# GpSimd subtracts the minimum and one exponential does two tiles, in a fused attention and MLP kernel

## The chip, the cores and the metric

The kernel runs on one core of one Trainium2 chip. The metric is the device time of one execution, in microseconds (us), as the median of several runs. A core has five engines that work side by side, each with its own queue of instructions, and that wait for each other through semaphores: TensorE (PE, matmuls; PEld is its loading of weights), VectorE (DVE), ScalarE (ACT), GpSimd (POOL) and SyncE (SP, here only an issuer of DMAs).

## The reference

A transformer block with 2048 tokens of width 640 that is modulated by a condition vector: attention with 32 heads of width 128 against a cache of 2048 keys and values, then a mixer and an MLP. Only the attention is touched by the change. Cut to it:

```
q = (x @ wq).reshape(B, Sq, H, Dh).transpose(0, 2, 1, 3)
scores = einsum('bhqd,bhkd->bhqk', q, k_cache) * Dh ** -0.5
p = softmax(scores, axis=-1)
o = einsum('bhqk,bhkd->bhqd', p, v_cache)
return o.transpose(0, 2, 1, 3).reshape(B, Sq, H * Dh) @ wo
```

The output projection, two layer norms, the mixer and the MLP follow. They are the same in both kernels.

## The kernel before, in words

The program is recorded operation by operation in a class `Prog`. Each operation names its engine, what it reads and what it writes; from that `Prog` derives the waits, also between two operations of one engine of which the second reads what the first wrote (VectorE, ScalarE, GpSimd). Each engine runs its operations strictly in the order in which they were recorded, so the order is the one written in the loop below.

The attention loop has one step `s` for each tile of 128 queries of one head: 16 tiles a head, 32 heads, 512 tiles. In one step:

- TensorE makes the scores of tile `s`, 128 x 2048, in two halves (`qk`, L301 and L15), into one PSUM area `Sps` of 2048 columns. There is no second such area: a half is made again for the next tile as soon as VectorE has read it. Between the halves TensorE multiplies the transposed probabilities of an earlier tile, `s - PVD`, by the values (`pv`, L314), and does a piece of other work: the next head's queries (`q_piece`, L246) or transposes of probabilities (`t_piece`, L262). Such pieces go into one of two PSUM banks in turn (`Oaug`, `QPp`). The list `PIECES` places the query pieces; `PE_STEPS` names the few tiles of a head whose probabilities TensorE transposes and from which step on (tiles 3 and 10 in a head of kind 0; tiles 2, 3 and 10 in kind 1, each fourth head). All others are transposed by a DMA (`transpose`, L231), mostly two tiles at a time.
- VectorE copies each half from PSUM into a score slot in SBUF (`negS`, L594), scaled by minus 1/sqrt(128), and keeps the minimum of each row. There are three slots: tile `s` uses slot `s % 3`, so it must wait until the reader of tile `s - 3` is done.
- GpSimd takes the smaller of the two halves' minima (L604, one column).
- ScalarE makes the probabilities in one instruction, exp(minimum - slot) with the minimum as its bias, from float32 into a bfloat16 ring of 10 tiles (`Pb`, L607).
- ScalarE also copies the product of two tiles out of PSUM (L585, in each second step), the queries (`q_evac`, L253) and the transposes made by TensorE (`t_evac`, L271). In each step these are recorded ahead of the exponential. `by_dve` gives the second half of some of the transposes to VectorE instead (L273): of tile 3 in every head, and of tile 2 in heads of kind 1, 40 copies in all.
- GpSimd takes reciprocals of the row sums for four tiles (`rcp`, L455), scales one tile (`norm`, L462), and for each fourth tile issues a DMA of the result to a scratch (L469).

`PVD` is the distance in steps between a tile's scores and its product with the values, 8 here. L585 is in the step in which the later tile of a pair has its product, an odd step with a `PVD` of 8. The line numbers are those of the profile of the kernel before; in the changed kernel lines behind the edits move down (L594 becomes L596, L604 L606, the plain exponential L619; the new pass is L610 and the new exponential L616).

The waits around the change are set by these keys of `Prog`:

```
r=[("S", half)], w=[("negS", s % 3), ("nmh", half, r8)])
...
r=[("negS", s % 3), ("nm", r8)], w=[("Pb", s % RP)])
```

The first is VectorE's copy into the slot, the second the exponential that reads it.

Of the kernel before, what the change touches and what calls it, by code (L numbers as in the profile page):

```python
# [7 lines left out]
ACT = mybir.ActivationFunctionType  # L8
# [115 lines left out]
def bass_adaLN_cond__mha_block_cached__mixer_s_mlp__prompt_kernel(  # L124
# [7 lines left out]
    NQT = SQ // 128  # L132
# [13 lines left out]
    with ExitStack() as es:  # L146
# [11 lines left out]
        if True:  # L158
            with ExitStack() as es1:
                sb1 = lambda name, shape, dt: es1.enter_context(nc.sbuf_tensor(name, shape, dt))  # L160
                RP = 10
                PVD = 8
                PE_STEPS = ({3: 6, 10: 13}, {2: 5, 3: 7, 10: 14})
                kind = lambda h: 1 if h % 4 == 1 else 0
                US = KT * (SQ + 4)
                sb1("pad", [128, 32], F32)
                ring = sb1("ring", [128, 2 * RP, SK], BF16)
                negS = sb1("negS", [128, 3, SK], F32)
                wo = sb1("wo", [128, H, D], BF16)
                kv = sb1("kv", [128, 2 * SK + 2 * NKT * 130 + 2 * KT * 128 + 2 * SQ], BF16)  # L170
                small = sb1("small", [128, 4 * NQT + 32], F32)
                hTx = sb1("hTx", [128, US], BF16)
                Of = sb1("Of", [128, 4, 2, 130], F32)
# [4 lines left out]
                nm0, nm1, nm, rl = [small[:, 4 * NQT + 8 * i:4 * NQT + 8 * i + 8] for i in range(4)]  # L178
# [8 lines left out]
                Pb = ring[:, 0:RP]  # L187
# [22 lines left out]
                G = Prog(nc, es1, "a")  # L210
# [61 lines left out]
                    else:  # L272
                        G.op("vector", lambda v: v.tensor_copy(dst, src), r=[("J", jb)], w=[("PT", g % RP, r)])  # L273

                by_dve = lambda g, r: r == 1 and g % NQT in (2, 3)
                PIECES = []
                for steps in PE_STEPS:
                    taken = [u for j in steps.values() for u in range(2 * j, 2 * j + 4)]
# [68 lines left out]
                if H > 1:  # L347
# [8 lines left out]
                     r=["id0"], w=["ident"])  # L356
# [3 lines left out]
                for k in range(KT):  # L360
                    G.op("gpsimd", lambda g, k=k: g.tensor_scalar(out=s_bc[:, k, :], in0=ones_f, scalar1=c_f[:, k:k + 1],
                                                                  scalar2=1.0, op0=ALU.mult, op1=ALU.mult),
                         r=["onesf", "cf"] + WRK, w=[("sbc", k)])
# [52 lines left out]
                def q_head0(cc):  # L416
                    for q in range(KT):
                        q_piece(0, cc, q)
                    q_evac(0, cc)
# [22 lines left out]
                def mod_rows(i):  # L442
                    n0, n1 = MROW[i]
                    bank = PO[:, (i % 2) * 512:(i % 2) * 512 + n1 - n0]

                    def f(t):
                        for k in range(KT):
                            ins = t.matmul(bank, s_bc[:, k, :], wmodr[:, k, n0:n1], start=(k == 0), stop=(k == KT - 1))
                        return ins
                    G.op("tensor", f, r=[("sbc", k) for k in range(KT)] + [("wm", 1)] + WRK, w=[("O", i % 2)])  # L450
                    G.op("scalar", lambda a: a.copy(mod_bc[:, n0:n1], bank), r=[("O", i % 2)], w=[("mod", i)])
# [35 lines left out]
                w2 = negb[:, 2 * H * 128:2 * H * 128 + KT * D].rearrange("p (k n) -> p k n", k=KT)  # L487
                us = hTx[:, 0:US].rearrange("p (k q) -> p k q", k=KT)
                nT = kv[:, 0:KT * SQ].rearrange("p (t k q) -> p t k q", t=NQT, k=KT)
# [61 lines left out]
                LAG = 4  # L551
                for s in range(NG + PVD + LAG):
                    h, j = divmod(s, NQT)
                    g_ = s - PVD
                    evacs = []
                    if s <= 2:
                        for i in ((0,), (1, 2), range(3, len(MROW)))[s]:
                            mod_rows(i)
                    if s == 3:
                        G.op("gpsimd", lambda g: g.tensor_scalar(  # L560
                            out=mod_bc[:, 2 * D:3 * D], in0=mod_bc[:, 2 * D:3 * D], scalar1=1.0, scalar2=1.0, op0=ALU.add, op1=ALU.mult),
                            r=[("mod", i) for i in range(len(MROW))], w=["mod"])
                    for half in range(2):
                        if s < NG:
                            qk(s, half)
                        if half == 0 and s in (NG + PVD - 5, NG + PVD - 4):
                            b0 = a_pe(0, None if s == NG + PVD - 5 else b0, (s - NG - PVD + 5,))
                        if half == 0 and s == NG + PVD - 2:
                            b1 = a_pe(1, None, (0,))
                        if 0 <= g_ < NG:  # L570
                            pv(g_, half)
                        if s == 0 and half == 1:
                            q_head0(NQC - 1)
                        if h + 1 < H and 2 * j + half in PIECES[kind(h)]:
                            cc, q = PIECES[kind(h)][2 * j + half]
                            q_piece(h + 1, cc, q)
                            if q == KT - 1:
                                evacs.append((q_evac, h + 1, cc))
                        for g, r in t_of(s):
                            t_piece(g, r, half)  # L580
                            if half == 1:
                                evacs.append((t_evac, g, r))
                    if 0 <= g_ < NG and g_ % 2 == 1:
                        p = g_ // 2
                        G.op("scalar", lambda a, p=p: a.copy(  # L585
                            Of[:, p % 4].rearrange("p z d -> p (z d)")[:, 0:259], PO[:, (p % 2) * 512:(p % 2) * 512 + 259]),
                            r=[("O", p % 2)], w=[("Of", p % 4)])
                    for fn, x, y in evacs:
                        if fn is q_evac or not by_dve(x, y):
                            fn(x, y)  # L590
                    for half in range(2):
                        if s < NG:
                            r8 = s % 8
                            G.op("vector", lambda v, half=half, s=s, r8=r8: v.tensor_scalar(  # L594
                                out=negS[:, s % 3, half * 1024:(half + 1) * 1024],
                                in0=Sps[:, half * 1024:(half + 1) * 1024],  # L596
                                scalar1=-SCALE, scalar2=None, op0=ALU.mult, op1=ALU.min,
                                accum_out=(nm0 if half == 0 else nm1)[:, r8:r8 + 1]),
                                r=[("S", half)], w=[("negS", s % 3), ("nmh", half, r8)])
                    for fn, x, y in evacs:  # L600
                        if fn is t_evac and by_dve(x, y):
                            fn(x, y)
                    if s < NG:
                        G.op("gpsimd", lambda g, r8=r8: g.tensor_scalar(  # L604
                            out=nm[:, r8:r8 + 1], in0=nm0[:, r8:r8 + 1], scalar1=nm1[:, r8:r8 + 1], scalar2=None, op0=ALU.min),
                            r=[("nmh", 0, r8), ("nmh", 1, r8)], w=[("nm", r8)])  # L606
                        G.op("scalar", lambda a, s=s, r8=r8: a.activation(  # L607
                            Pb[:, s % RP, :], negS[:, s % 3, :], ACT.Exp, bias=nm[:, r8:r8 + 1], scale=-1.0),
                            r=[("negS", s % 3), ("nm", r8)], w=[("Pb", s % RP)])
                        if not is_pe(s):  # L610
                            if s % 2 == 1 and not is_pe(s - 1):
                                transpose(s - 1, 2)
                            elif s % 2 == 1 or is_pe(s + 1):
                                transpose(s, 1)
                        if j == 2 and h >= 1 and h + 1 < H:
                            load_k(h + 1)  # L616
                        if h + 1 == H and j in (2, PVD + 1):
                            i = 0 if j == 2 else 1
                            load_ot(0, OTC[i], OTC[i + 1], i)  # L619
                        if j == 6 and h + 2 < H:  # L620
                            load_wq(h + 2)
                        if j == PVD + 1 and h + 1 < H:
                            load_v(h + 1)
                    if 0 <= s - PVD - LAG:
                        gr, z = divmod(s - PVD - LAG, 4)
                        if z == 0:
                            rcp(gr)
                        norm(gr, z)
                    if s == NG:
                        G.op("gpsimd", lambda g: g.memset(mhalf, -0.5), w=["mhalf"] + NEG)  # L630
                        load_ot(0, OTC[2], OTC[3], 2)
                        load_xt(0, 1)
                        load_ot(1, 0, H // 2, 0)
                        load_ot(1, H // 2, H, 1)
                    if s == NG + 2:
                        load_xt(1, NQC)
# [57 lines left out]
                for n in range(KT):  # L694
                    lst = []
                    p = 0
                    while p < 128:
# [8 lines left out]
                        p = pe_  # L706
# [203 lines left out]
```

## Time and profile before

| | before |
|---|---|
| median of 3 runs | 1574.27 us |
| lowest, highest run | 1574.03, 1575.15 us |
| profiled execution: span, first to last instruction | 1568.9 us |
| busy, TensorE matmuls | 1472.3 us (94%) |
| busy, TensorE weight loads | 923.4 us (59%) |
| busy, VectorE | 1398.3 us (89%) |
| busy, ScalarE | 1275.9 us (81%) |
| busy, GpSimd | 623.0 us (40%) |
| mean granted TensorE clock | 0.998 |
| first and last L594 | start at 35.4 and 1250.6 us |

The profile is of one execution on the chip. For the profiled execution the record holds its span alone, from its first instruction to its last; the median of the runs is 5.4 us longer, and this rest lies around the span. The shares are means over the whole span: the attention loop takes it up to about 1252 us, and the output projection, the mixer and the MLP, in which ScalarE is nearly idle, take what is left. Neighbouring instructions of one engine overlap by some tenths of a microsecond, so what an instruction costs its engine is the distance between two starts rather than its own duration. A group's line ends with the idle time of its engine just before such instructions, and with what ended that idle time.

### The profile page before, as it was taken

Reading aid. Unit: us, or ns where it says so; the run is one execution under the profiler, and the core shown is the slowest. Engines: PE = TensorE matmul, PEld = TensorE weight load, DVE = VectorE, ACT = ScalarE, POOL = GpSimd, SP = SyncE. Lnnn points to the kernel's source line nnn. Section 1 sums busy time; section 2 is a strip of 40 time slices with the busy share of each in tenths; the row PEclk is TensorE's granted clock in tenths of the full one; section 3 lists DMA queues with packets and bytes.
Section 4 is the critical chain, followed back from the end, with each engine's and each line's share of the span. In section 5 each row is a group of like instructions: output and inputs, shape, how many; then the busy total and the mean of one; then the engine's idle time right before and its main releaser. Section 6 shows DMA issues by size and latency. Waiting matters only on the chain.

```text
span 1568.9 us, 33553 instructions
## 1 busy us (share of the span) xinstructions
PE 1472.3 (94%) x13947; PEld 923.4 (59%) x13175; DVE 1398.3 (89%) x2471; ACT 1275.9 (81%) x1121; POOL 623.0 (40%) x1396
## 2 busy tenths in 40 slices
PE   5899999999999999999999999999999899999999
PEld 3466666666665566566656666566566655554545
DVE  6999999999999999999999999999999937667435
ACT  4999999999999999999999999999999900034230
POOL 0144444444444444444444444444444433323100
PEclk9999999999999999999999999999999999999999
DMA  9999999999999999999999999999999999725100
GB/s 298 239 221 239 237 242 237 233 241 243 237 240 233 239 232 232 240 236 235 229 237 236 233 243 249 226 242 243 235 241 237 238 246 190 157 53 144 38 22 34
DMA packets 1172828, 334.59 MB, mean 213 GB/s; under 512 B 1153280, under 2 KB 1166656, under 8 KB 1172672
## 3 DMA queue, kind: packets, MB, share of 16 engines
q1 hardware_dynamic: 1164192, 311.30, 100.8%
q0 software_dynamic: 6144, 16.79, 3.5%
q10 hardware_dynamic: 2336, 4.34, 0.8%
q8 instruction: 108, 1.77, 0.5%
q14 instruction: 48, 0.39, 0.1%
HBM read 43.48 MB, written 19.40 MB: 40 GB/s over the span
## 4 chain that ended last, share of the span: by engine, by line
ACT 40%; DVE 23%; PE 19%; DMA 9%; issue 7%; POOL 1%; POOLq 0%; DVEq 0%
ACT ring L607 32%; DVE negS L594 20%; DMA ring<-ring 8%; PE Sps L540 8%; PE Sps L847 4%; ACT ring L271 3%; ACT kv L253 2%; ACT Of L585 2%; PE QPp L798 2%; PE Oaug L798 2%; DVE ring L273 1%; PE Sps L783 1%; DVE ring L379 1%; DMA negS<-o_scratch 1%; PE PTp L314 1%
## 5 line engine op out<-in xcount | busy, mean ns | idle before, releaser
L594 DVE TENSOR_SCALAR_CACHE_REDUCE negS<-Sps 128x1024 f32<-128x1024 f32 x1024 | 1177.7, 1224 | 19.4 <-PE Sps L15 18.5
L607 ACT ACTIVATE ring<-negS,small 128x2048 bf16<-128x2048 f32 x512 | 1045.7, 2066 | 13.7 <-POOL small L604 12.5
L314 PEld LDWEIGHTS PTp<-kv,ring 128*128 128x128 bf16 x8192 | 554.1, 98 | 325.0 <-issue 69.6
L314 PE MATMUL PTp<-kv,ring 128*128 128x129 bf16 x8192 | 645.3, 220 | 25.0 <-DMA ring<-ring 23.9
L15 PE MATMUL Sps<-kv 128*128 128x512 bf16 x1024 | 387.9, 379 | 16.8 <-DVE negS L594 9.9
L604 POOL TENSOR_SCALAR small<-small 128x1 f32<-128x1 f32 x512 | 146.4, 286 | 621.8 <-DVE negS L594 621.7
L301 PE MATMUL Sps<-kv 128*128 128x512 bf16 x919 | 354.3, 386 | 27.8 <-DVE negS L594 16.5
L462 POOL TENSOR_SCALAR On<-Of,small 128x128 bf16<-128x128 f32 x512 | 191.0, 373 | 13.0
L301 PEld LDWEIGHTS Sps<-kv 128*128 128x128 bf16 x1024 | 98.1, 96 | 141.7 <-DVE negS L594 121.6
L455 POOL TENSOR_TENSOR small<-Of,small 128x4 f32<-128x4 f32 x128 | 133.1, 1040 | 8.8 <-ACT Of L585 8.7
L469 POOL DMA_DIRECT2D o_scratch<-On x128 | 103.1, 806 | 40.8 <-POOL On L462 37.2
L585 ACT COPY Of<-PTp 128x259 f32<-128x259 f32 x256 | 108.6, 424 | 13.2 <-PE PTp L314 13.2
L246 PE MATMUL Oaug<-hTx,kv 128*128 128x512 bf16 x268 | 101.9, 385 | 3.7 <-DVE hTx L411 3.7
L246 PE MATMUL QPp<-hTx,kv 128*128 128x512 bf16 x259 | 97.7, 382 | 2.6 <-ACT hTx L406 2.1
L728 ACT ACT_TABLE_LOAD x1 | 1.3, 1283 | 112.6 <-POOL hTx L746 112.6
L594 DVE DVE_READ_ACCUMULATOR negS<-Sps 128x1 f32 x1024 | 90.3, 88 | 0.0
L271 ACT COPY ring<-Oaug 128x1024 bf16<-128x1024 bf16 x72 | 77.0, 1069 | 0.0
L641 POOL TENSOR_SCALAR negS<-negS 128x1 f32<-128x1 f32 x48 | 24.2, 504 | 125.2 <-DVE negS L650 125.2
L540 PE MATMUL Sps<-wo,negS 128*128 128x128 bf16 (+1 forms) x503 | 69.9, 298 | 1.2 <-DMA negS<-o_scratch 0.8
L540 PE MATMUL Sps<-wo,hTx 128*128 128x512 bf16 (+1 forms) x502 | 69.3, 297 | 0.5
L851 DVE TENSOR_TENSOR ring<-Sps,ring 128x640 f32<-128x640 f32 x15 | 12.4, 824 | 59.5 <-PE Sps L847 59.5
L655 DVE TENSOR_TENSOR ring<-Sps,mod_bc 128x640 f32<-128x640 f32 x16 | 13.1, 821 | 53.6 <-PE Sps L540 32.9
(88 smaller groups left out, 1052.7 us busy)
## 6 DMA issues: line engine op xcount, KB each, us to landing
kv<-in_A_v_cache_dram SPq DMA_DIRECT2D x32, 512.0 KB, 5.0
o_scratch<-On POOLq DMA_DIRECT2D x128, 128.0 KB, 4.7
kv<-in_A_wq_dram SPq DMA_DIRECT2D x32, 160.0 KB, 3.2
wo<-in_A_wo_dram SPq DMA_DIRECT2D x1, 5120.0 KB, 16.5
ring<-ring SPq DMA_TRANSPOSE x248, 7.1
ring<-in_A_x_dram SPq DMA_DIRECT2D x5, 640.0 KB, 6.6
ring<-in_w_mod_dram SPq DMA_DIRECT2D x1, 3200.0 KB, 13.8
out_dram<-wo SPq DMA_DIRECT2D x15, 160.0 KB, 1.8
```

The costliest lines, as they stand in the source:

```text
L15: return t.add_instruction(mybir.InstMatmult(name=t.bass.get_next_instruction_name(), ins=[t.lower_ap(rhs), t.lower_ap(lhsT)], outs=[t.low ...
L246: G.op("tensor", lambda t: t.matmul(JB[jb], wq[:, hb, q, :], hT[:, q, cc * 512:(cc + 1) * 512], start=(q == 0), stop=(q == KT - 1)), r=[(" ...
L271: G.op("scalar", lambda a: a.copy(dst, src), r=[("J", jb)], w=[("PT", g % RP, r)])
L301: ins = (t.matmul if c2 == 0 else partial(same_weights, t))(Sps[:, col:col + 512], QT[:, hb, j * 128:(j + 1) * 128], KTs[:, hb, col:col + ...
L314: ins = t.matmul(ob[:, 0:129], PTs[:, b, kt, :], Vaug[:, hb, kt, 0:129], start=(kt == 0), stop=(kt == NKT - 1))
L455: G.op("gpsimd", lambda g: g.tensor_tensor(out=rl[:, 4 * b:4 * b + 4], in0=Of[:].rearrange("p a z d -> p (a z) d")[:, 4 * b:4 * b + 4, 128 ...
L462: G.op("gpsimd", lambda g: g.tensor_scalar(out=On[:, b, z, :], in0=Of[:, 2 * b + z // 2, z % 2, 0:128], scalar1=rl[:, 4 * b + z:4 * b + z ...
L540: ins = t.matmul(YB[b][:, c0:c0 + cw], OTj[pr % 2][:, 2 * hh + z, :], wo[:, hh, c0:c0 + cw], start=(hh == 0), stop=(hh == H - 1))
L585: G.op("scalar", lambda a, p=p: a.copy(Of[:, p % 4].rearrange("p z d -> p (z d)")[:, 0:259], PO[:, (p % 2) * 512:(p % 2) * 512 + 259]), r= ...
L594: G.op("vector", lambda v, half=half, s=s, r8=r8: v.tensor_scalar(out=negS[:, s % 3, half * 1024:(half + 1) * 1024], in0=Sps[:, half * 102 ...
L604: G.op("gpsimd", lambda g, r8=r8: g.tensor_scalar(out=nm[:, r8:r8 + 1], in0=nm0[:, r8:r8 + 1], scalar1=nm1[:, r8:r8 + 1], scalar2=None, op ...
L607: G.op("scalar", lambda a, s=s, r8=r8: a.activation(Pb[:, s % RP, :], negS[:, s % 3, :], ACT.Exp, bias=nm[:, r8:r8 + 1], scale=-1.0), r=[( ...
```

## The change

Of the 16 tiles of each head, eight (four pairs that begin with tiles 0, 4, 8 and 12) get their probabilities in another way. GpSimd subtracts the minimum from the score slot over 128 x 2048 and writes the difference as bfloat16 to the place in the ring where the probabilities belong. After the second tile of a pair, one ScalarE instruction does the exponential of both tiles in place, over 4096 columns, without a bias operand. The other eight tiles keep their exponential. `PVD` goes from 8 to 9, with which L585 comes in even steps, and `norm` and `rcp` come one step later. `by_dve` keeps 16 of its 40 copies on VectorE (tile 2 in heads of kind 1, tile 3 in heads with `h % 4 == 3`); 24 become copies of ScalarE.

```diff
-                PVD = 8
+                PVD = 9
                 PE_STEPS = ({3: 6, 10: 13}, {2: 5, 3: 7, 10: 14})
                 kind = lambda h: 1 if h % 4 == 1 else 0
+                MERGED = (0, 4, 8, 12)
+                merged = lambda s: s % NQT // 2 * 2 in MERGED
...
-                by_dve = lambda g, r: r == 1 and g % NQT in (2, 3)
+                by_dve = lambda g, r: r == 1 and (g % NQT == 2 or g % NQT == 3 and g // NQT % 4 == 3)
...
-                        G.op("scalar", lambda a, s=s, r8=r8: a.activation(
-                            Pb[:, s % RP, :], negS[:, s % 3, :], ACT.Exp, bias=nm[:, r8:r8 + 1], scale=-1.0),
-                            r=[("negS", s % 3), ("nm", r8)], w=[("Pb", s % RP)])
+                        if merged(s):
+                            G.op("gpsimd", lambda g, s=s, r8=r8: g.tensor_scalar(
+                                out=Pb[:, s % RP, :], in0=negS[:, s % 3, :], scalar1=nm[:, r8:r8 + 1], scalar2=1.0,
+                                op0=ALU.subtract, op1=ALU.mult),
+                                r=[("negS", s % 3), ("nm", r8)], w=[("Pb", s % RP)])
+                            if s % 2 == 1:
+                                pair = ring[:, (s - 1) % RP:s % RP + 1].rearrange("p r s -> p (r s)")
+                                G.op("scalar", lambda a, pair=pair: a.activation(pair, pair, ACT.Exp, scale=-1.0),
+                                     w=[("Pb", (s - 1) % RP), ("Pb", s % RP)])
+                        else:
+                            G.op("scalar", lambda a, s=s, r8=r8: a.activation(
+                                Pb[:, s % RP, :], negS[:, s % 3, :], ACT.Exp, bias=nm[:, r8:r8 + 1], scale=-1.0),
+                                r=[("negS", s % 3), ("nm", r8)], w=[("Pb", s % RP)])
```

## The prediction

> **What bounds the kernel now.** I first read the table of windows, then the groups of instructions by line, then the timeline of each engine in one head. Columns of the windows: stretch, its length, busy time (and instructions) of TensorE, its weight loads, VectorE, ScalarE, GpSimd, then granted clock, DMA share, GB/s.
>
> ```profile
> 700.00:750.00 50.00, 47.93 (x493) 31.57 (x458) 50.00 (x90) 49.72 (x41) 22.45 (x52) 1.00 1.24 236
> ```
>
> VectorE and ScalarE are both full through the whole attention stage; GpSimd is less than half busy. The groups say what fills them:
>
> ```profile
> L594 DVE TENSOR_SCALAR_CACHE_REDUCE negS<-Sps 128x1024 f32<-128x1024 f32 x1024 | 1177.7, 1224 | 19.4 <-PE Sps L15 18.5 <-ACT ring L607 0.2
> L607 ACT ACTIVATE ring<-negS,small 128x2048 bf16<-128x2048 f32 x512 | 1045.7, 2066 | 13.7 <-POOL small L604 12.5
> ...
> L462 POOL TENSOR_SCALAR On<-Of,small 128x128 bf16<-128x128 f32 x512 | 191.0, 373 | 13.0
> L604 POOL TENSOR_SCALAR small<-small 128x1 f32<-128x1 f32 x512 | 146.4, 286 | 621.8 <-DVE negS L594 621.7
> ```
>
> L594 scores run from 35.4 to 1251.9 us of the span, 1216.5 us. The reader should see how little VectorE waits for ScalarE: 0.2 us in all, although each L594 pair writes one of only three score slots, which the exponential of three tiles earlier must have read. That is the cover to watch. Busy times overlap, so I price instructions by start-to-start pitch. On VectorE:
>
> ```profile
> 58.06 0.69 DVE L273 COPY ring<-QPp 128x1024 bf16<-128x1024 bf16 x1
> 58.66 1.22 DVE L594 TENSOR_SCALAR_CACHE_REDUCE negS<-Sps 128x1024 f32<-128x1024 f32 x1
> 59.80 0.08 DVE L594 DVE_READ_ACCUMULATOR negS<-Sps 128x1 f32 x1
> 59.80 1.22 DVE L594 TENSOR_SCALAR_CACHE_REDUCE negS<-Sps 128x1024 f32<-128x1024 f32 x1
> ```
>
> A half tile advances 1.145 us, a tile 2.29, a copy 0.60. Check: 512 x 2.29 + 40 x 0.605 + 20 idle = 1216.5. On ScalarE, columns start, duration, instruction:
>
> ```profile
> 720.84 2.02 ACT L607 ACTIVATE ring<-negS,small 128x2048 bf16<-128x2048 f32 x1
> 722.75 0.38 ACT L585 COPY Of<-PTp 128x259 f32<-128x259 f32 x1
> 723.00 1.04 ACT L271 COPY ring<-QPp 128x1024 bf16<-128x1024 bf16 x1
> 723.91 2.04 ACT L607 ACTIVATE ring<-negS,small 128x2048 bf16<-128x2048 f32 x1
> ```
>
> Pitches: exponential 1.90 (it ends 2.05 after its start), L585 0.25, L271 0.90; L253, read the same way, 0.47.
>
> **What the change does to the loads.** VectorE loses 24 copies of 0.605, 14.5 us, and they go to ScalarE at 0.90, 21.6 us. ScalarE replaces 256 exponentials (two of 1.90 a pair) by 128 of 4096 columns. From 259 to 1024 columns the copies' pitch grows 0.65 us, 0.84 ns a column, so 2048 more cost 1.72; a pointer operand less saves 0.09 (L406, with two of them, takes 780 ns, L802, with none, 597, both 512 columns). Pair: 1.90 + 1.72 - 0.09 = 3.53 us. New loads: ScalarE 256 x 1.90 + 128 x 3.53 + 256 x 0.25 + 128 x 0.90 + 128 x 0.47 = 1178 us; VectorE 1172.5 + 16 x 0.605 = 1182 us. By loads alone the stage would shrink by 14.5 us. But the loads do not decide.
>
> **The price of the new pass.** No GpSimd row has 2048 columns. From below: a straight line through L462 (128 columns, 373 ns) and L560 (640 columns, 726 ns) gives 0.69 ns a column and 1.69 us. From above: sixteen L462 of their pitch 0.35 make 5.6 us. L560 has constants where the new pass reads a pointer, so its fixed part may be the smaller, and the line too flat; the same engine's memsets of bfloat16 (206 ns at 128, 366 at 320, 632 at 640) grow 0.83 ns a column. I take 0.373 + 1920 x 0.00083 = **1.97 us**, close to the lower end since a long row has its fixed part once.
>
> A rule that speaks against this: the Trainium skill, GPSIMD Engine Reference, section 3.1, gives about 1.8 cycles an element at 1.2 GHz as the best case. Worked out from it, an estimate of 3.07 us for the elements alone; in place of 1.97 this would lift the sum below to some 2050 us. The trace disagrees at 640 columns, where that rule would ask for 0.96 us and L560 took 0.73.
>
> **The new wait.** Tiles 0,1 of each four are merged, 2,3 are not, and there are three slots: tile 5 overwrites tile 2's slot, so L594 of tile 5 waits for tile 2's exponential. On ScalarE that one now stands behind the pair's, which waits for tile 1's GpSimd pass. Steps are counted from the end of L594 of tile 1 (the end of its accumulator read), hops from the rows where one engine visibly waited for another:
>
> - 0.10 hop, L604 0.28, 0.11 until its reader on GpSimd starts (as L455 to L462), pass 1.97, 0.04 hop: the pair starts at 2.50 (a plain exponential starts at 0.42 now).
> - pair 3.53: 6.03. L585, which the deeper pipeline puts on even tiles, 0.25: 6.28.
> - any L253 or L271 of that step, then tile 2's exponential to its end 2.05: 8.33; hop 0.04 (as L384 to L388).
> - L594 of tile 5, two halves and the accumulator read, 2.37: 10.74.
>
> So tile 1 to tile 5 takes 10.74 us where VectorE alone needs 9.16. Behind the waiting L594 stand its own next tiles; behind those TensorE's scores, which need the PSUM half emptied, and GpSimd. The excess goes away only if the pass and the evacuations together cost under 0.39 us.
>
> The evacuations land in the chain. In the 24 heads with kind 0, L253 at step 2 (0.47), L271 at 6 (0.90), L253 at 10 (0.47), L271 at 14 (0.90); in the 8 heads of kind 1, 0.47 at step 2 and 0.90 at 14 (at step 6 VectorE does it). Kind 0 by groups of four: 11.21, 11.64, 11.21, 11.64.
>
> One knot more, counted from the end of tile 5 in kind 0. TensorE's query piece of step 8 needs the bank that L271 of step 6 empties at 6.28 + 1.07 = 7.35. It stands ahead of tile 8's second score half. So that half is ready at 8.2 (a piece 0.22, two score matmuls 0.61), and tile 8 ends at 9.48 rather than 6.87; tile 9 ends at 11.77 rather than 11.64. GpSimd then has tile 8's L604 and pass, L462, and L469's issue before tile 9's L604:
>
> ```profile
> 1252.19 0.38 POOL L462 TENSOR_SCALAR On<-Of,small 128x128 bf16<-128x128 f32 x1
> 1252.86 0.81 POOL L469 DMA_DIRECT2D o_scratch<-On  x1 [0.29 <-POOL On L462]
> ```
>
> That is 0.10 + 0.28 + 0.11 + 1.97 + 0.34 + 0.29 + 0.81 = 3.90, so tile 9's L604 starts at 13.38, not 11.87: 1.51 more for the third group. (In the other groups 3.90 behind tile 4 comes just before tile 5's end.) A kind 0 head: 11.21 + 11.77 + 11.21 + 1.51 + 11.64 = 47.34. Kind 1, the same way: its step 6 has no ScalarE evacuation, but its query piece of step 9 waits for L271 of step 7, 11.38; then 10.74; and the knot sits at its end: 11.21 + 11.38 + 10.74 + 11.77 + 1.51 = 46.61.
>
> **The sum.** 24 x 47.34 + 8 x 46.61 = 1509 us; plus the 8 us that VectorE loses in the first three tiles, less 2.5 in the last head, which prepares no next one, plus 1 for the pipeline's ninth tile: 1515 against 1216.5, so +298. The profiled span of 1568.9 becomes 1867; the median of the runs, 5.4 us above the span, becomes **1870 us**. The DMA transposes start later, by some 6 us against nine tiles of about 2.9 us each until their product: hidden; without that cover TensorE would wait out L231's 7.1 us. After attention nothing is changed.
>
> Each 0.1 us in the chain costs about 13 us, in the pass about 17, since the knot counts it again. A pass of 1.69 gives about 1824; one of 2.4 about 1940; hops and pitches may err by 0.2 together, 30 us.
>
> **The rivals.**
> - *The ring covers the delay: faster.* Merged slots are freed by GpSimd, 2.46 us after L594, and ScalarE has less to do. If VectorE were never held, the 14.5 us are gained: about 1560. For it: both loads fall, and VectorE waits only 0.2 us for ScalarE now. Against it: tile 2's slot is not freed by GpSimd. It decides from a pass under 0.39 us; a row of 640 columns already takes 0.73. Chance 0.05; 0.02 for a draw, within 0.2% (what a measurement of this kernel can tell from no change).
> - *The pass is slow.* Twice the lower line's cost per column (1.37 ns) gives 3.09 us: 1.12 more, about five times a head, 179 us: 2050; sixteen full blocks would make GpSimd the bound, at two passes and 5.0 us of its other rows a group, 16.2 x 128, near 2430. For it: no row is longer than 640. Against it: three sizes grow slowly. Chance 0.08. The skill's rule would be this case.
> - *A small stall.* A pass of 1.69 and no knot give 44.6 and 43.2 us a head, 1780; with hops 0.2 shorter in each of the 128 groups, 1755. Chance 0.05 for less than 1770.
> - *The change does not do what it says*: the built order holds 256 passes and 128 exponentials of 4096 columns, so I give this nothing.
>
> The forecast has 0.80 with 1770 to 2000, which spans passes from 1.69 to about 2.7 us. Slower 0.93, same 0.02, faster 0.05.
>
> **What would show it.** VectorE's busy share in attention falls to about 80%, and L594's idle time names L619, the plain exponential, some 200 us and more; ScalarE waits for the pass L610 before most pairs, 1 to 3 us each. The pass shows near 1.97 us, the pair near 3.6. After every fourth tile VectorE has a gap of 1.5 us or more, the longest near tile 8. If L594 shows no gap the reasoning is wrong; if the gap is there with another size, the pass is the first suspect.

## The result and the profile after

| | before | after |
|---|---|---|
| median | 1574.71 us (4 runs beside those of after) | 2999.39 us (4 runs, 2998.56 to 2999.87) |
| ratio | | 1.904, 95% interval 1.901 to 1.908 |
| span of the profiled execution | 1568.9 us | 2997.8 us |
| stage of the scores, first to last L594 or L596 | 1216.5 us | 2632 us |
| mean granted TensorE clock | 0.998 | 0.780 |

The kernel is slower, as forecast, but by 1425 us and not by 296. (A profiled execution of the changed kernel took 1.9 us more than its span, 2999.69 against 2997.8; so of the 5.4 us by which the median before lies above its span, only about this much lies around the span, and the rest is the difference of one execution from another.) The costliest groups of the changed kernel (line, engine, operation, tiles, count | busy us, mean ns | idle before, and who ended it):

```profile
L596 DVE TENSOR_SCALAR_CACHE_REDUCE negS<-Sps 128x1024 f32<-128x1024 f32 x1024 | 1215.1, 1223 | 1405.6 <-POOL ring L610 737.9 <-ACT ring L619 370.9 <-PE Sps L15 290.0
L610 POOL TENSOR_SCALAR ring<-negS,small 128x2048 bf16<-128x2048 f32 x256 | 1842.2, 7196 | 23.9
L616 ACT ACTIVATE ring<-ring 128x4096 bf16<-128x4096 bf16 x128 | 462.9, 3617 | 1436.9 <-POOL ring L610 1436.9
L606 POOL TENSOR_SCALAR small<-small 128x1 f32<-128x1 f32 x512 | 149.8, 293 | 173.6 <-DVE negS L596 168.0
```

The pass L610 takes 7.20 us where the prediction put 1.97, and both engines that were full before now wait: VectorE idles 1406 us ahead of L596, ScalarE 1437 us ahead of the pair. All of ScalarE's wait ends with the pass. Of VectorE's, 738 us end with the pass itself, which holds the slot of a merged tile, and only 371 with the plain exponential L619, the wait that the prediction had foreseen. A thousand microseconds of the stage, in the table of windows (columns as in the prediction), show GpSimd busy for 91%, VectorE and ScalarE below half, and a granted clock of 0.75:

```profile
200.00:1200.00 1000.00, 579.40 (x4579) 340.99 (x4188) 467.10 (x785) 451.24 (x338) 909.54 (x580) 0.75 0.52 109
```

GpSimd's timeline (start, duration, instruction) shows the queue: behind a first tile's pass stand L464 and L471, then the next tile's L606, then the next pass.

```profile
1006.71 7.21 POOL L610 TENSOR_SCALAR ring<-negS,small 128x2048 bf16<-128x2048 f32 x1
1013.89 0.37 POOL L464 TENSOR_SCALAR On<-Of,small 128x128 bf16<-128x128 f32 x1
1014.56 0.82 POOL L471 DMA_DIRECT2D o_scratch<-On  x1 [0.29 <-POOL On L464]
1015.43 0.32 POOL L606 TENSOR_SCALAR small<-small 128x1 f32<-128x1 f32 x1
1015.84 7.18 POOL L610 TENSOR_SCALAR ring<-negS,small 128x2048 bf16<-128x2048 f32 x1
```

Two passes, 14.4 us, and the 5.0 of other rows that the prediction counted make 19.4 us for four tiles, 2480 us for the stage. It took 2632. GpSimd waited 168 us for VectorE (L606 above), which is about the rest.

### The profile page after: what moved, and what is told of

It reads as the page before. It is cut to its first block, busy times and chain, and to the rows that moved or that the text cites. A ratio compares the mean times of both kernels' runs of the same rounds, so it can differ in the third digit from the quotient of the medians.

```text
span 2997.8 us, 33903 instructions
## 1 busy us (share of the span) xinstructions
PE 1837.6 (61%) x14199; PEld 1065.2 (36%) x13175; DVE 1427.7 (48%) x2447; ACT 1271.3 (42%) x1017; POOL 2467.1 (82%) x1652
## 4 chain that ended last, share of the span: by engine, by line
POOL 77%; PE 12%; ACT 5%; issue 4%; DVE 2%; DMA 0%; POOLq 0%; DVEq 0%
POOL ring L610 61%; POOL On L464 5%; PE Sps L542 5%; POOL small L606 4%; ACT ring L616 4%; POOL o_scratch L471 3%; POOL small L457 3%; PE Sps L859 2%; PE Oaug L810 1%; PE QPp L810 1%; ACT ring L273 1%; PE Oaug L248 1%; DVE negS L596 1%; PE Sps L795 0%; PE Sps L15 0%
## 5 line engine op out<-in xcount | busy, mean ns | idle before, releaser
L596 DVE TENSOR_SCALAR_CACHE_REDUCE negS<-Sps 128x1024 f32<-128x1024 f32 x1024 | 1215.1, 1223 | 1405.6 <-POOL ring L610 737.9
L610 POOL TENSOR_SCALAR ring<-negS,small 128x2048 bf16<-128x2048 f32 x256 | 1842.2, 7196 | 23.9
L616 ACT ACTIVATE ring<-ring 128x4096 bf16<-128x4096 bf16 x128 | 462.9, 3617 | 1436.9 <-POOL ring L610 1436.9
L316 PEld LDWEIGHTS PTp<-kv,ring 128*128 128x128 bf16 x8192 | 673.9, 113 | 680.6 <-issue 574.4
L316 PE MATMUL PTp<-kv,ring 128*128 128x129 bf16 x8192 | 778.7, 249 | 172.2 <-ACT Of L587 172.2
L303 PE MATMUL Sps<-kv 128*128 128x512 bf16 x1024 | 477.3, 466 | 602.3 <-DVE negS L596 599.7
L619 ACT ACTIVATE ring<-negS,small 128x2048 bf16<-128x2048 f32 x256 | 504.2, 2007 | 0.0
L15 PE MATMUL Sps<-kv 128*128 128x512 bf16 x1024 | 472.2, 461 | 0.0
L248 PE MATMUL Oaug<-hTx,kv 128*128 128x512 bf16 x320 | 154.6, 487 | 325.2 <-ACT ring L273 322.3
L606 POOL TENSOR_SCALAR small<-small 128x1 f32<-128x1 f32 x512 | 149.8, 293 | 173.6 <-DVE negS L596 168.0
L464 POOL TENSOR_SCALAR On<-Of,small 128x128 bf16<-128x128 f32 x512 | 189.9, 371 | 13.0
L248 PEld LDWEIGHTS Oaug<-hTx,kv 128*128 128x128 bf16 x320 | 37.4, 117 | 337.4 <-ACT ring L273 242.0
L471 POOL DMA_DIRECT2D o_scratch<-On x128 | 104.9, 820 | 40.8 <-POOL On L464 37.2
L264 PE MATMUL Oaug<-ident,ring 128*128 128x128 bf16 x576 | 77.2, 277 | 40.3 <-ACT ring L619 40.3
L587 ACT COPY Of<-PTp 128x259 f32<-128x259 f32 x256 | 93.2, 365 | 16.8 <-PE PTp L316 16.8
L596 DVE DVE_READ_ACCUMULATOR negS<-Sps 128x1 f32 x1024 | 85.5, 83 | 0.0
L273 ACT COPY ring<-Oaug 128x1024 bf16<-128x1024 bf16 x72 | 72.9, 1012 | 7.0 <-PE Oaug L264 7.0
```

Source lines behind the costliest of these rows:

```text
L15: return t.add_instruction(mybir.InstMatmult(name=t.bass.get_next_instruction_name(), ins=[t.lower_ap(rhs), t.lower_ap(lhsT)], outs=[t.low ...
L248: G.op("tensor", lambda t: t.matmul(JB[jb], wq[:, hb, q, :], hT[:, q, cc * 512:(cc + 1) * 512], start=(q == 0), stop=(q == KT - 1)), r=[(" ...
L303: ins = (t.matmul if c2 == 0 else partial(same_weights, t))(Sps[:, col:col + 512], QT[:, hb, j * 128:(j + 1) * 128], KTs[:, hb, col:col + ...
L316: ins = t.matmul(ob[:, 0:129], PTs[:, b, kt, :], Vaug[:, hb, kt, 0:129], start=(kt == 0), stop=(kt == NKT - 1))
L464: G.op("gpsimd", lambda g: g.tensor_scalar(out=On[:, b, z, :], in0=Of[:, 2 * b + z // 2, z % 2, 0:128], scalar1=rl[:, 4 * b + z:4 * b + z ...
L606: G.op("gpsimd", lambda g, r8=r8: g.tensor_scalar(out=nm[:, r8:r8 + 1], in0=nm0[:, r8:r8 + 1], scalar1=nm1[:, r8:r8 + 1], scalar2=None, op ...
```

## The experiments

**1. What does the pass cost by itself?** Behind the end of the kernel before, GpSimd runs 31 instructions on scratch tiles, one at a time, of which the pass is one:

```diff
+                Z.op("gpsimd", lambda g: g.tensor_scalar(out=db[:, 0:128], in0=src[:, 0:128], scalar1=sc, scalar2=1.0, op0=ALU.subtract, op1=ALU.mult), ...
+                Z.op("gpsimd", lambda g: g.tensor_scalar(out=db[:, 0:2048], in0=src[:, 0:2048], scalar1=sc, scalar2=1.0, op0=ALU.add, op1=ALU.mult), ...
...
```

> The kernel before, with 30 GpSimd instructions on scratch tiles behind its end, each alone on the chip and each waiting for the one ahead of it: subtract-and-multiply with a pointer operand, float32 to bfloat16, at 1 to 2048 columns; multiply-and-multiply of the same shape; add-and-multiply; one operation alone; float32 out; constants for the pointer; a plain copy; bfloat16 in. Three theories for the 7.20 us of the pass L610. Form: subtraction is slow at any length, some 3.5 ns a column, so 128 columns take 0.7 us and multiply-and-multiply at 2048 columns takes 1.7 to 2.0. Length: all forms follow the straight line of L464 and L562 up to some length and bend beyond it, so multiply-and-multiply at 2048 takes 7.2 as well. Contention: the pass is slow only beside the other engines' traffic, so every form here takes 1.7 to 2.0 us at 2048 columns.

Timeline of GpSimd in that run. L894, L899, L901: subtract, then multiply, at 128, 640 and 2048 columns; L902, L905, L907: multiply twice at 128, 640 and 2048; L908: add, then multiply; L909, L910: one operation, subtract or multiply; L919: add and multiply with constants; L920: a plain copy; L921: subtract and multiply from bfloat16.

```profile
1570.60 0.72 POOL L894 TENSOR_SCALAR ring<-negS,small 128x128 bf16<-128x128 f32 x1
...
1577.22 2.42 POOL L899 TENSOR_SCALAR ring<-negS,small 128x640 bf16<-128x640 f32 x1
...
1583.54 7.16 POOL L901 TENSOR_SCALAR ring<-negS,small 128x2048 bf16<-128x2048 f32 x1
1590.80 0.38 POOL L902 TENSOR_SCALAR ring<-negS,small 128x128 bf16<-128x128 f32 x1
...
1592.64 0.81 POOL L905 TENSOR_SCALAR ring<-negS,small 128x640 bf16<-128x640 f32 x1
...
1594.76 1.98 POOL L907 TENSOR_SCALAR ring<-negS,small 128x2048 bf16<-128x2048 f32 x1
1596.83 1.97 POOL L908 TENSOR_SCALAR ring<-negS,small 128x2048 bf16<-128x2048 f32 x1
1598.90 5.45 POOL L909 TENSOR_SCALAR ring<-negS,small 128x2048 bf16<-128x2048 f32 x1
1604.44 5.45 POOL L910 TENSOR_SCALAR ring<-negS,small 128x2048 bf16<-128x2048 f32 x1
...
1626.70 1.90 POOL L919 TENSOR_SCALAR ring<-negS 128x2048 bf16<-128x2048 f32 x1
1628.67 1.89 POOL L920 CAST ring<-negS 128x2048 bf16<-128x2048 f32 x1
1630.66 7.16 POOL L921 TENSOR_SCALAR ring<-ring,small 128x2048 bf16<-128x2048 bf16 x1
```

The theory of the form holds; the other two fall. Subtract-and-multiply costs 7.16 us with the chip otherwise still, so the traffic of other engines has hardly a part in the 7.20, and its cost grows evenly from 128 columns on: (7.16 - 0.72) / 1920 = 3.35 ns a column. Multiply-and-multiply grows by 0.83 ns, (1.98 - 0.38) / 1920. Add-and-multiply is as cheap. It is not subtraction alone: one operation, be it subtract or multiply, costs 5.45. Subtract-and-multiply from bfloat16 costs the same 7.16. So what decides here is which operations the instruction does. (The run as a whole took 1639.91 us, the scratch instructions included.)

**2. The chain with a short pass.** From the eleventh tile on the pass covers 128 columns in one run, 640 in another.

```diff
-                                out=Pb[:, s % RP, :], in0=negS[:, s % 3, :], ...
+                                out=Pb[:, s % RP, 0:128 if s >= RP else SK], in0=negS[:, s % 3, 0:128 if s >= RP else SK], ...
```

> The changed kernel, but from the eleventh tile on the pass covers only the first 128 of 2048 columns; the other columns keep what was there, so that part of the computation is left out. Everything else, waits included, is as in the changed kernel. The pass then takes 0.37 us (or 0.7, if subtraction is slow at any length). If the pass's price was the only step that failed, the chain of the prediction with 0.37 in place of 1.97 holds: four tiles take 9.14 us plus the evacuations, a head 39.3 (kind 0) or 38.6, so about 1620 us, and about 1670 with 0.7. If the wait on the slot costs something in itself, by an engine clock or a hop that is priced too low, it takes over 1700.

> As the run with 128 columns, with 640 columns of the pass. By the straight line of L464 and L562 the pass takes 0.73 us and the run some 1670 us. If subtraction costs 3.5 ns a column at any length, the pass takes 2.3 to 2.5 us and the run, by the chain, about 1930. The difference of the two cut runs over the difference of their passes, some 4 to 5 times 32 heads, 130 to 170 us for each us of the pass, is the chain's slope.

They took 1713.19 and 1996.34 us, one run each (before: 1567.39 on that chip). The short passes took 0.75 and 2.45 us. Six passes at the start are full, which the expectations left out; if each delays everything behind it by what it takes more than a short one (an estimate from the 7.16, 0.72 and 2.42 us above), they add 39 and 28 us. With them the chain gives about 1709 and 1958. The first is 4 us below the run, the second 38 us, and where these 38 come from was not followed. The six full passes are the same in both runs, so they drop out of the slope: (1996.34 - 1713.19) / (2.45 - 0.75) = 167 us for each us on 250 of the 256 passes, about 170 for all of them; the prediction had 170.

**3. The other parts of the change alone.** No tile is merged; the depth of 9 and the moved copies stay.

```diff
-                MERGED = (0, 4, 8, 12)
+                MERGED = ()
```

> The other parts of the change alone: the pipeline depth of 9 and 24 copies moved from VectorE to ScalarE, with a plain exponential for every tile. ScalarE's pitches add up to 512 x 1.90 + 256 x 0.25 + 128 x 0.90 + 128 x 0.47 = 1212 us, VectorE's to 1182, against 1192 and 1197 before: the bound moves to ScalarE and the time stays within 15 us of before, 1570 to 1590. If these parts carry a loss of their own (evacuations that come late to TensorE) it takes over 1600.

1576.33 us against 1567.39, ratio 1.0048 (1.0036 to 1.0061): a small loss, in which VectorE waits 12.9 us for the exponential in place of 0.2. Of the loss of 1425 us all but these 9 are the merging's.

**4. The pass in its cheap form.** The same 256 passes, but they add minus the minimum:

```diff
-  ... scalar1=nm1[:, r8:r8 + 1], scalar2=None, op0=ALU.min),
+  ... scalar1=nm1[:, r8:r8 + 1], scalar2=-1.0 if merged(s) else 1.0, op0=ALU.min, op1=ALU.mult),
...
-                                op0=ALU.subtract, op1=ALU.mult),
+                                op0=ALU.add, op1=ALU.mult),
```

> The changed kernel with the pass in the form that took 1.97 us alone: L606 gives minus the minimum for merged tiles, and the pass adds it. The same work, 256 passes of 1.97 in place of 7.20. If the chain through the slot of tile 2 and ScalarE's order is as the prediction has it, and only the pass was mis-priced, this run comes out near the forecast, 298 us above before: 1865 to 1885. From the two cut runs, 1713 less 39 for their first six full passes plus 166 x 1.25, it is 1881. If only GpSimd's load had made the loss, four tiles would cost it 2 x 1.97 + 4.98 = 8.9 us, less than VectorE's 9.5, and the time would be that of before within 20 us.

1884.62 us against 1575.75 for before, ratio 1.196 (1.194 to 1.198): 309 us more, where the prediction's chain had 298. The stage took 1524 us, forecast 1515. VectorE's wait now ends at the plain exponential, here L620:

```profile
L596 DVE TENSOR_SCALAR_CACHE_REDUCE negS<-Sps 128x1024 f32<-128x1024 f32 x1024 | 1191.4, 1221 | 324.8 <-ACT ring L620 199.1 <-PE Sps L15 124.8
```

One group of four in that run, ScalarE first and then the VectorE row that waits:

```profile
807.23 3.62 ACT L617 ACTIVATE ring<-ring 128x4096 bf16<-128x4096 bf16 x1 [3.35 <-POOL ring L611]
810.76 0.36 ACT L587 COPY Of<-PTp 128x259 f32<-128x259 f32 x1
811.01 0.59 ACT L255 CAST kv<-Oaug 128x512 bf16<-128x512 f32 x1
811.49 3.90 ACT L620 ACTIVATE ring<-negS,small 128x2048 bf16<-128x2048 f32 x2
```

```profile
813.63 1.23 DVE L596 TENSOR_SCALAR_CACHE_REDUCE negS<-Sps 128x1024 f32<-128x1024 f32 x1 [1.31 <-ACT ring L620]
```

These are the steps of the prediction in their order: the pair's pitch 3.53, L587 0.25, L255 0.48, then the exponential of tile 2 (the first of the two in the row), and 0.1 us behind its end VectorE's tile 5. The pair's own start is not quite as forecast: at 807.23 it lies 3.0 us behind the end of tile 1's scores (804.23), not 2.5. Nor is VectorE's other wait accounted for piece by piece: 125 us ended with TensorE's scores, 19 before the change. The prediction has such a wait, the knot at tile 8, but no run measures it by itself.

**5. Take the slot's wait away by order.** On top of experiment 4, the pair's exponential and its transpose are recorded behind the two plain exponentials that follow.

```diff
-                            if s % 2 == 1:
-                                pair = ring[:, (s - 1) % RP:s % RP + 1] ...
...
+                            if s % 4 == 3:
+                                pair = ring[:, (s - 3) % RP:(s - 2) % RP + 1] ...
+                                transpose(s - 3, 2)
```

> The add run, but the pair's exponential (and its DMA transpose) is recorded two tiles later, behind the plain exponentials of the two tiles that follow, so that nothing stands between L596 of tile 2 and the exponential that frees its slot but what stood there before. If the slot's wait is the cause of the loss, it goes: VectorE needs 1202 us with its idle start, ScalarE 1178, so 1550 to 1590. If the loss comes from elsewhere, by a TensorE bank, by GpSimd's backlog or by the transposes that now start even later, the time stays above 1700.

> add_late with all 40 copies on VectorE as before the change. Loads: VectorE 1172 + 24 + 20 idle = 1217 as before, ScalarE 1192 - 36 = 1156. If add_late is bound by VectorE, this one is 10 to 15 us slower than add_late; if add_late is bound by ScalarE's order or by late transposes, it is the same or faster.

1869.78 and 1873.39 us: hardly any gain, so the first part of that expectation failed. The slot's wait did go, but others took its place. VectorE's and TensorE's groups:

```profile
L596 DVE TENSOR_SCALAR_CACHE_REDUCE negS<-Sps 128x1024 f32<-128x1024 f32 x1024 | 1191.3, 1221 | 305.5 <-PE Sps L15 272.8 <-ACT ring L616 30.5 <-POOL ring L611 1.1
...
L316 PE MATMUL PTp<-kv,ring 128*128 128x129 bf16 x8192 | 678.8, 227 | 193.4 <-DMA ring<-ring 150.9 <-ACT Of L587 42.3
```

VectorE waits 31 us for ScalarE in place of 199, but 273 for TensorE in place of 125, and TensorE waits 151 for transposes that start too late for a product nine tiles on. The copies' place makes hardly a difference (4 us, where a bound by VectorE's load would have cost 10 to 15), so VectorE's load is not the bound.

> add_late one tile deeper (10 between scores and product; the scaling still 13 behind, as there). In add_late VectorE's wait on the exponential was gone (30 us in place of 199) but TensorE waited 151 us for DMA transposes, and VectorE 273 for TensorE. If the late transposes are all that is left, one tile more (2.4 us) takes most of that away: 1600 to 1680. If the banks are the cause, it stays at 1870.

With `PVD = 10` and `LAG = 3` (`LAG` is the distance in steps between a tile's product and its scaling) it is 1824.18 us: the wait of TensorE's products for DMAs falls from 151 to 47 us, VectorE's for TensorE from 273 to 205. Better, and still not what was expected: TensorE now waits 138 us for L255 to empty a bank, 78 in the run before. From its table of waits (who waited for whom: us in total, times, longest):

```profile
PE QPp L264 <- ACT kv L255: 137.7, 61, 3.7
PE PTp L316 <- DMA ring<-ring: 46.6, 26, 4.3
```

**6. The same order with the slow pass.** As in 5, with the pass of 7.20 us:

> The changed kernel with its slow subtracting pass of 7.20 us, in the later order of add_late. GpSimd's rows for four tiles: two passes 14.4 and 4.98 of other work, 19.4 us x 128 = 2480 us. If GpSimd's queue is the bound of the changed kernel, the order hardly helps: 2480 + 352 outside of the scores = 2830 to 2900. If the waits through the slot and ScalarE are the bound there as well, it falls to less than 2500.

2839.45 us (one run), the stage 2469: the sum of GpSimd's rows, 2480. GpSimd now hardly waits for VectorE any more, 15 us in place of 168:

```profile
L606 POOL TENSOR_SCALAR small<-small 128x1 f32<-128x1 f32 x512 | 148.5, 290 | 20.6 <-DVE negS L596 15.0
```

So in the changed kernel GpSimd's queue sets the time, and the waits that come back to it through ScalarE, TensorE and VectorE add the 160 us above that.

**7. Take the slot's wait away by a fourth slot, then GpSimd's backlog, then the banks.** One change on top of the other, starting from the kernel of experiment 4.

```diff
-   negS[:, s % 3, :]
+   NS(s % 4)
```

The fourth slot lies in the place of the last seven heads of `wo`, which are loaded after the last score; `NS(i)` is slot `i`.

> The add run with a fourth score slot (in the place of the last seven heads of the output weights, which are loaded after the last score instead of at the start). Tile 5 then overwrites tile 1's slot, which GpSimd frees early; tile 6 overwrites tile 2's. If tile 2's slot is what holds VectorE, its wait on the plain exponential falls from 199 us to under 60. What is late next is GpSimd's queue: tile 0's pass, L464 and L471 keep tile 1's minimum until 3.9 us after tile 0, so the pair starts 6.3 us behind tile 0 and tile 2's exponential ends some 13 us behind it with an evacuation: about 10 us for four tiles, 1640 to 1690 us. If the slot's wait is not the cause, the time stays at 1870 to 1890.

With it the late load moves one step:

```diff
-                LAG = 4
+                LAG = 5
```

> add_slots4 with the scaling of the results one step later, so that L471's DMA issue stands behind the second tile's pass and not between the two. GpSimd then starts tile 1's minimum 0.4 us late and not 1.5: the pair starts 2.9 us behind tile 1, tile 2's exponential is done before tile 6 needs its slot, or 0.5 us late where an evacuation stands ahead of it. If slot and queue are the two causes, nearly all of the loss goes: 1570 to 1610. If TensorE's banks or the transposes also hold it, 1640 or more.

```diff
-                PE_STEPS = ({3: 6, 10: 13}, {2: 5, 3: 7, 10: 14})
+                PE_STEPS = ({3: 7, 10: 14}, {2: 5, 3: 7, 10: 14})
...
+                by_dve = lambda g, r: r == 0 or g % NQT == 2
```

> add_slots4_lag5, in which VectorE no longer waits for the slot but TensorE still waits 141 us for ScalarE (92 for a plain exponential whose tile it is to transpose, 48 for a bank that an evacuation empties late) and its clock falls after such stalls. Two things are moved: in heads of kind 0 the transposes by TensorE start one step later (tiles 3 and 10 at steps 7 and 14), and VectorE takes the first half of all of them and both halves of tile 2, 80 copies in all. Loads: VectorE 1172 + 48 + 20 = 1240 us, ScalarE 1178 - 58 = 1120. If these two waits are what was left of the loss, 1590 to 1650 us; if something else holds the kernel there, 1720 or more.

| | us | before beside it | ratio (95%) |
|---|---|---|---|
| fourth slot | 1841.07 | 1568.09 | 1.174 (1.172 to 1.176) |
| and L471 behind the second pass | 1757.08 | 1568.09 | 1.119 (1.115 to 1.123) |
| and the banks | 1634.30 | 1571.02 | 1.040 (1.038 to 1.042) |

With the fourth slot VectorE no longer waits for the exponential, but the loss over the kernel before falls only from 309 to 273 us, where a fall of some 200 us was expected. What was late next was GpSimd's backlog, 84 us; the expectation that this would take nearly all of the rest failed too. Then TensorE's waits for ScalarE, 123 us; with them the mean granted clock rose from 0.971 to 0.991, and no run parts the one from the other. Only this last step came out as expected. VectorE's idle time ahead of L597 is 34 us there:

```profile
L597 DVE TENSOR_SCALAR_CACHE_REDUCE negS<-Sps 128x1024 f32<-128x1024 f32 x768 | 895.8, 1220 | 32.3 <-PE Sps L15 31.3
L597 DVE TENSOR_SCALAR_CACHE_REDUCE wo<-Sps 128x1024 f32<-128x1024 f32 x256 | 304.1, 1219 | 1.5 <-PE Sps L15 1.4
```

Of the 63 us that are left, 44 lie in the stage (1261 us against 1216.5): 40 more copies on VectorE than before the change are 24 us by their pitch, and VectorE waits some 14 us more for TensorE. 18 us lie behind the last score (335 us to the end of the span, against 317), where TensorE waits 12 us for the output weights that are now loaded late:

```profile
L543 PE MATMUL Sps<-wo,hTx 128*128 128x512 bf16 (+1 forms) x512 | 73.0, 304 | 12.4 <-DMA wo<-in_A_wo_dram 12.4
```

No version here beats the kernel before.

## Why the prediction was wrong

- **What bounds the kernel** was right: VectorE and ScalarE by load, with the slots as the cover.
- **The loads** were right. The pair's pitch is 3.52 to 3.53 us (priced 3.53); the depth and the moved copies alone change the time by 0.5%.
- **The price of the new pass** is the step that failed: "I take **1.97 us**, close to the lower end since a long row has its fixed part once". It is 7.20, above even the upper end of 5.6. The reasoning about columns was right to 0.01 us for the rows that it came from: multiply-and-multiply and add-and-multiply at 2048 columns take 1.98 and 1.97. But L462 multiplies twice and L560 adds and multiplies, and the pass subtracts, then multiplies; no GpSimd row of the kernel before subtracts. I took a price by engine and size from other operations and let the operation go. The bound from above failed for the same reason: sixteen blocks of the right operation are 16 x 0.72 = 11.5 us, not 5.6.
- **What follows from it.** The case was among the rivals as "the pass is slow", with GpSimd as the bound at two passes and 5.0 us a group. With 7.20 that sentence gives 2480 us for the stage, and with the slow pass in the later order the stage took 2469, in the order of the change 2632. It had 0.08, and only up to 5.6 us.
- **The figure that the prediction took from the Trainium skill**, 1.8 cycles an element as the best case (GPSIMD Engine Reference, section 3.1), fits neither form here: 0.83 ns is 1.0 cycle at its 1.2 GHz, 3.35 ns is 4.0. The rejection by L560 was right for the additions and said nothing of the subtraction.
- **The chain** was right in size: with a pass of 1.97 us the loss was 309 us against 298, VectorE's wait on the plain exponential 199 us ("some 200 us and more"), the slope about 170 us as forecast. (Two slips do not bear on this: 1867 + 5.4 is 1872 and not 1870, and the range's lower end of 1770 is not a pass of 1.69 us, for which the prediction itself has 1824, but about that pass without the knot.) How closely the sum agrees may be luck in part: the pair started 0.5 us later than forecast, TensorE's clock was at 0.96, which is in no term, and the pass of 2.45 us took 38 us more than the chain gives. It was too simple in one respect: the wait on the slot is one of several that lie close behind each other (GpSimd's backlog, the banks, the transposes), so to take it away alone brought only 15 us by order and 36 by a fourth slot.
- **"The transposes are hidden"** held in the order of the change: no DMA is among the larger waits of experiment 4. It held narrowly: recorded two tiles later, in experiment 5, they were a wait of 151 us.
- **Not foreseen**: TensorE's clock, below.

## What to carry to other kernels

Price an instruction from a row of the same operation, not only of the same engine, shape and type; where there is none, say so and let the range go by the dearest operation of that engine, or measure it first. Between a change of load and a change of time stand the buffers: a merged instruction delays what stands behind it on its engine, and with three slots the delay reaches the engine that fills them three tiles later. When one such wait is taken away, look for the next; here there were three more behind the first.

## What the runs showed of the hardware

GpSimd's `tensor_scalar` over 2048 columns took 1.97 us for add-and-multiply or multiply-and-multiply, 5.45 us for one operation alone, and 7.16 us for subtract-and-multiply. To write the subtraction as an addition of the negated operand was worth 1115 us to this kernel (2999.39 against 1884.62). Why the forms differ no run here shows.

TensorE's granted clock halved after a stall. In the run with the fourth slot and `LAG = 5`, TensorE:

```profile
817.46 0.38 PE L15 MATMUL Sps<-kv 128*128 128x512 bf16 x1
817.67 0.63 PE L317 MATMUL PTp<-kv,ring 128*128 128x129 bf16 x8
821.72 0.63 PE L304 MATMUL Sps<-kv 128*128 128x512 bf16 x1 [3.41 <-ACT ring L274]
822.14 0.63 PE L15 MATMUL Sps<-kv 128*128 128x512 bf16 x1
```

The matmul of 512 columns behind an idle time of 3.4 us takes 0.63 us, and 0.38 before it. The windows of that run give the granted clock (third from the end):

```profile
815.00:818.00 3.00, 3.00 (x38) 2.02 (x33) 3.00 (x5) 2.37 (x4) 2.66 (x4) 1.00 0.99 215
818.00:822.00 4.00, 0.59 (x7) 0.26 (x5) 1.25 (x4) 4.00 (x4) 2.18 (x5) 0.78 1.01 217
822.00:824.00 2.00, 2.00 (x12) 1.17 (x10) 1.19 (x2) 2.00 (x3) 0.00 (x0) 0.50 1.26 287
824.00:826.00 2.00, 2.00 (x12) 1.17 (x10) 1.09 (x3) 2.00 (x2) 1.76 (x2) 0.50 0.63 143
826.00:828.00 2.00, 2.00 (x14) 0.93 (x11) 1.08 (x3) 0.16 (x1) 0.85 (x2) 0.73 0.52 119
828.00:830.00 2.00, 1.95 (x22) 1.23 (x19) 2.00 (x5) 0.00 (x0) 1.47 (x2) 1.00 1.27 289
```

It is 0.50 for some five microseconds of work and then 1.00 again, so a stall that begins elsewhere can cost TensorE a slow stretch on top. The Trainium skill, TensorE: Matmul & The Clock Gate, Part 1, has it that TensorE is let down to half its clock after an idle window of about 3.4 us and up again after as long a busy one; these rows agree in the half, but not in the two lengths. The idle time begins at 818.30; 0.78 over 818 to 822 means that the clock fell at about 820.2, 1.9 us later, and 0.73 over 826 to 828 that it rose at about 827.1, 5.4 us after work began. Nor is 3.4 us a sharp limit: in the changed kernel an idle time of 3.74 us left the next matmul of 512 columns at 0.39 us.

```profile
363.72 0.39 PE L303 MATMUL Sps<-kv 128*128 128x512 bf16 x1 [3.74 <-DVE negS L596]
```

In the changed kernel, whose stalls are up to 11 us (TensorE's longest wait for L273), the mean clock of the whole execution is 0.78.
